# Agent attention with a mixture of experts on one core: maxima over partitions by TensorE, scores and routing products later in TensorE's order, keys spread over three quarters of a batch, low halves on GpSimd

## The chip, the cores and the metric

The kernel runs on one core of a Trainium2 chip. The metric is the device time of one execution in microseconds (us), the median over several runs. A core has five engines that each work through a queue of their own in order: TensorE (PE in the rows; PEld is its weight load), VectorE (DVE), ScalarE (ACT), GpSimd (POOL) and SyncE (SP, which here issues nearly all DMAs). They wait for each other by semaphores.

## The reference

```python
def attn(q, k, v, agents):              # q, k, v: (4, 11456, 128); agents: (4, 49, 128)
    scale = 1 / sqrt(128)
    a2k = softmax(scale * agents @ k.T)     # each agent over all 11456 keys
    agent_v = a2k @ v
    q2a = softmax(scale * q @ agents.T)     # each query over the 49 agents
    return q2a @ agent_v                    # x: 4*11456 = 45824 tokens of 128

def moe(x, expert_emb, tau, w1, w2):    # 8 experts, w1 (8, 128, 1024), w2 (8, 1024, 128)
    logits = normalize(x) @ normalize(expert_emb).T / tau
    e = argmax(logits); gate = softmax(logits)[e]
    return gate * (relu(x @ w1[e]) @ w2[e])   # top 1
```

All inputs and the output are float32 in DRAM.

## The kernel before

**Units and steps.** A batch of 11456 tokens is cut into 12 units of 1024 tokens (128 partitions by 8 columns; the last unit is 96 by 2). Two tiles of 512 tokens make a unit, 23 tiles a batch. The expert network (FFN) takes a tile in 8 slices of 128 of its 1024 hidden channels. A slice of a tile is a **step**: 184 steps a batch, 736 in all. In step i TensorE makes the hidden slice `hp` by two fp16 products (L698, L699: high and low part of the weights, 512 columns each), ScalarE writes its rectified high half `hh` (L702), VectorE the low half `hl` (L703), and four steps later (LAG) twelve products of 128 columns bring `hh` and `hl` into the output `yp` (L720 to L722). After eight steps VectorE multiplies `yp` by the gate (`ot`, L735) and SP stores it (L741).

**Key, value and query units** are worked beside the steps. `split` (L278) prepares a key or query unit: ScalarE squares and sums it (L284), VectorE makes a power of two from the sum (`half_scale`, `hsc`, L158 to L162), then the unit is written as a high and a low fp16 half, and SP transposes both by DMA (L299) into `kT` or `qT`. The high half is made by ScalarE (L291) or, in the way "P" of `LO_BY`, by GpSimd (L289). The low half is made by VectorE in one operation (L296) or, in the way "p", by GpSimd in two (L293, L294). While the FFN runs, keys take the ways p, d, P in turn, and queries p and P. `scores` (L302) then makes 24 small products (tile `sp`, 49 columns each). For a key unit ScalarE copies the scores to `s_u` (L338) and VectorE brings them into the running maximum `m_run` (L342). When all twelve are done, `k_max` (L396) takes the maximum over a partition's columns (VectorE, L399) and then over the partitions (`allred`, GpSimd, L135: tile `pm`). `k2_unit` then subtracts `pm` (`kd`, L382: by VectorE in the first batch, by GpSimd in the later ones), takes the exponential on ScalarE (L384), and TensorE sums the values by it (`avp`, L388). A query unit goes from its scores through L545, L547, an exponential (L549), two fp16 halves (L553, and `e` on GpSimd, L554) and a DMA transpose (L556) to `tt`, the tile that both the routing products (`rtp`, L565) and the FFN read. `rt`, `quad` and `nrm` (L590 to L622) give the tokens' norms and gates.

**Order.** Each unit is a generator; a number that it yields is a delay in steps. `spawn` starts one, `keys` (L993) starts the key and value units of batch b+1 while batch b is in the FFN (the table `W_` gives the stretches of a batch in which keys and values are started), `queries` (L1031) starts one query unit for every two tiles, four units ahead. The tile framework's scheduler then puts the emitted instructions into an order for each engine, with the FFN's at higher priority. Input units lie in the pool `ld` (8 buffers), split and transposed units in three buffers each (`xs`, `xT`). The first batch's keys, values and four queries come before step 0 (`first`), and of the keys every second unit is worked in fp32. Before step 0 no unit of the ways p and P is made. The expert of a batch is chosen on the chip from its first query unit (`e0i`), and SP reads it into a register before it loads the weights (`load_expert`, L526): all DMAs that stand behind in SP's queue wait for that.

Of the kernel before, what the change touches and what calls it, by code (L numbers as in the profile page):

```python
# [31 lines left out]
def kernel(ctx: ExitStack, tc: tile.TileContext, q, k, v, agents, emb, tau, w1, w2, out):  # L32
# [35 lines left out]
    ld = ctx.enter_context(tc.tile_pool(name="ld", bufs=8))  # L68
# [63 lines left out]
    def allred(col, n, tag, op=ROP.max, bufs=2):  # L132

        r = sm.tile([P, n], F32, name="pm", tag=tag, bufs=bufs)
        pool.partition_all_reduce(r, col, P, op)  # L135
        return r
# [37 lines left out]
    def now_run(g):  # L174

        while True:
            try:
                next(g)
            except StopIteration as s:
                return s.value  # L180

# [3 lines left out]
    sga, isga = now_run(pow2(allred(amx, 1, "amxr"), 10, "sga"))  # L185
# [92 lines left out]
    def split(kind, b, u, g):  # L278

        s = units[kind, b, u]  # L280
        p, n = ushape(u)
        sq = sm.tile([P, 1], F32, name="usq", tag=kind + "usq", bufs=3)[:p]
        xs = wk.tile([P, UJ, 2, D], F16, name=kind + "s", tag="xs", bufs=3)
        act.activation(xs[:p, :n, 0], s[:p, :n], AF.Square, accum_out=sq)  # L284
        yield g
        sc, iv = yield from half_scale(sq, 14, kind + "u", 4, escale if kind == "q" else None)
        lo = LO_BY[kind][u % len(LO_BY[kind])] if ffn_at[0] is not None else "d"
        if lo == "P":
            pool.tensor_tensor(out=xs[:p, :n, 0], in0=s[:p, :n], in1=sc.unsqueeze(2).broadcast_to([p, n, D]), op=ALU.mult)  # L289
        else:  # L290
            act.activation(xs[:p, :n, 0], s[:p, :n], AF.Copy, scale=sc)  # L291
        if lo == "p":
            pool.tensor_tensor(out=s[:p, :n], in0=s[:p, :n], in1=sc.unsqueeze(2).broadcast_to([p, n, D]), op=ALU.mult)  # L293
            pool.tensor_tensor(out=xs[:p, :n, 1], in0=s[:p, :n], in1=xs[:p, :n, 0], op=ALU.subtract)  # L294
        else:
            dve.scalar_tensor_tensor(out=xs[:p, :n, 1], in0=s[:p, :n], scalar=sc, in1=xs[:p, :n, 0],  # L296
                                     op0=ALU.mult, op1=ALU.subtract)
        xT = wk.tile([P, 2 * UJ, P], F16, name=kind + "T", tag="xT", bufs=3)
        sp.dma_start_transpose(out=xT[:, : 2 * n, :p], in_=xs[:p, :n].rearrange("p c h d -> p (c h d)"))  # L299
        return xT, iv  # L300
# [27 lines left out]
    def k1_unit(b, u, g, cp):  # L328
        kb = blk_of(b, u)
        p, n = ushape(u)  # L330
        while ("k", b, u) not in units:
            yield 1
        xT, iv = yield from split("k", b, u, g[0])
        yield g[1]
        spv = scores(b, u, xT)
        st = wk.tile([P, UJ, A], F32, name="s_u", tag="s_u", bufs=NU)[:p, :n]
        if cp is act:
            act.activation(st, spv, AF.Copy, scale=iv)  # L338
        else:
            dve.tensor_scalar(st, spv, iv, None, ALU.mult)  # L340
        yield g[2]
        dve.tensor_tensor(out=kb.m_run[:p, :n, :], in0=kb.m_run[:p, :n, :], in1=st, op=ALU.max)  # L342
        kb.s[u] = st
        kb.k1 += 1

    def k1_f32(b, u):
# [4 lines left out]
        kT = wk.tile([P, 2 * UJ, P], F16, name="kT", tag="xT", bufs=3).rearrange("k c p -> k (c p)").bitcast(F32)  # L351
# [15 lines left out]
        act.activation(st, s[:p, : n * A].rearrange("p (c a) -> p c a", a=A), AF.Copy, scale=sga[:p])  # L367
        dve.tensor_tensor(out=kb.m_run[:p, :n, :], in0=kb.m_run[:p, :n, :], in1=st, op=ALU.max)
# [27 lines left out]
    def k_max(b, i=0):  # L396
# [3 lines left out]
        kb.m = allred(m1, A, "kmax", bufs=max(2, NB))  # L400
# [543 lines left out]
    def first():  # L944
# [11 lines left out]
        for kind, b, u in ops:  # L956
# [7 lines left out]
            if kind == "k":  # L964
                if not hasattr(batches[b], "blks"):
                    k_start(b)
                spawn(k1_f32(b, u) if b == 0 and u in KF else k1_unit(b, u, (0, 1, 0), act))
# [9 lines left out]
            elif kind == "m":  # L977
# [4 lines left out]
                k_max(0, i)  # L982
# [10 lines left out]
    def keys():  # L993
# [3 lines left out]
        W_ = [(0, 0.2, 0.2, 0.7), (-0.2, 0.0, 0.3, 0.85), (-0.2, 0.0, 0.3, 0.85)]  # L997
# [8 lines left out]
        for i, (at, kind, b, u) in enumerate(ops):  # L1006
# [104 lines left out]
```

## Time and profile before

| | |
|---|---|
| median of 3 runs | 1204.39 us (1203.04 to 1204.79) |
| the profiled execution: its time, its span | 1205.41 us, 1203.6 us |
| PE busy, mean granted clock | 86%, 0.958 of full speed |
| DVE, ACT, POOL busy | 75%, 57%, 36% |
| share of the 16 DMA engines | 55% |
| step 0 of the FFN | about 110 us after the start |

The rows further down come from the trace of the profiled execution; their times count from the start of its span. A row of a timeline ends with the idle time of the engine just before that instruction and, behind an arrow, the instruction whose end it waited for. [...]

### The profile page before, as it was taken

The numbers are of one execution on the slowest core, as the hardware profiler recorded it, in microseconds if no ns is written. First come the engines' busy times: TensorE is split into PE (matmuls) and PEld (weight loads), VectorE is DVE, ScalarE is ACT, GpSimd is POOL, SyncE is SP. The second block draws the span as 40 slices with busy tenths as digits, with TensorE's granted clock in tenths as the row PEclk, the third lists the DMA queues.
The fourth block names the chain that finished last, engine by engine and source line by source line (L and its number), as shares of the span: only waits on it lengthen the run. The fifth ranks groups of instructions, "written<-read, shape, count | busy, mean of one in ns | idle before, by whom it ended". The sixth has DMA issues, their size and how long they took to land. (4 is left out here: it accounts for less than half of the span.)

```text
span 1203.6 us, 34100 instructions
## 1 busy us (share of the span) xinstructions
PE 1036.3 (86%) x13877; PEld 844.2 (70%) x13877; DVE 903.1 (75%) x2103; ACT 686.9 (57%) x1304; POOL 430.0 (36%) x409
## 2 busy tenths in 40 slices
PE   2666876698999877799998987689999989999998
PEld 2664655577787765587887776568788867877776
DVE  2555787567688896788778887686778998777785
ACT  2434676455647765555755676555554575655553
POOL 2002665445401644733442343733331262252200
PEclk9887898899999999899999999899999999999999
DMA  4976999465225988554542699753330382241100
GB/s 143 249 143 209 226 200 206 106 159 128 68 60 199 205 202 192 123 119 111 140 137 54 151 236 204 158 98 96 100 73 28 91 208 68 93 92 46 39 37 32
DMA packets 302697, 157.35 MB, mean 131 GB/s; under 512 B 227067, under 2 KB 279371, under 8 KB 302539
## 3 DMA queue, kind: packets, MB, share of 16 engines
q1 hardware_dynamic: 302475, 155.16, 54.4%
q8 instruction: 109, 1.79, 0.6%
q14 instruction: 49, 0.40, 0.1%
q0 software_dynamic: 64, 0.00, 0.0%
HBM read 75.80 MB, written 23.53 MB: 83 GB/s over the span
## 5 line engine op out<-in xcount | busy, mean ns | idle before, releaser
L703 DVE SCALAR_TENSOR_TENSOR hl<-hp,hh 128x512 f16<-128x512 f32 (+1 forms) x736 | 475.5, 666 | 95.9 <-ACT hh L702 86.2
L702 ACT ACTIVATE hh<-hp 128x512 f16<-128x512 f32 (+1 forms) x736 | 414.8, 584 | 217.0 <-PE yp L721 95.1
L720 PE MATMUL yp<-w2h,hh 128*128 128x128 f16 (+1 forms) x2880 | 528.5, 222 | 6.2 <-DVE ot L735 6.2
L721 PE MATMUL yp<-w2l,hh 128*128 128x128 f16 (+1 forms) x2880 | 529.0, 222 | 1.9 <-DVE w2l L516 1.9
L722 PE MATMUL yp<-w2h,hl 128*128 128x128 f16 (+1 forms) x2880 | 528.8, 222 | 0.0
L698 PE MATMUL hp<-tt,gh 128*128 128x512 f16 (+1 forms) x736 | 277.8, 378 | 66.1 <-DVE hl L703 60.4
L720 PEld LDWEIGHTS <-hh 128*128 128x128 f16 (+1 forms) x2880 | 288.0, 100 | 50.8 <-issue 3.3
L722 PEld LDWEIGHTS <-hl 128*128 128x128 f16 (+1 forms) x2880 | 287.8, 100 | 49.8 <-issue 6.2
L721 PEld LDWEIGHTS <-hh 128*128 128x128 f16 (+1 forms) x2880 | 288.1, 100 | 46.3 <-issue 8.5
L699 PE MATMUL hp<-tt,gl 128*128 128x512 f16 (+1 forms) x736 | 278.0, 378 | 0.3 <-DVE gl L507 0.3
L699 PEld LDWEIGHTS <-gl 128*128 128x128 f16 x736 | 72.0, 98 | 78.3 <-issue 73.1
L591 POOL TENSOR_TENSOR rt<-rt,qe 128x392 f32<-128x392 f32 (+1 forms) x48 | 49.7, 1036 | 158.6 <-ACT rt L590 158.6
L388 PE MATMUL avp<-vt,kd 128*98 128x129 f32 x720 | 98.1, 282 | 7.8 <-issue 7.8
L554 POOL TENSOR_TENSOR e<-qe,e 128x392 f16<-128x392 f32 (+1 forms) x48 | 41.7, 868 | 175.3 <-DVE e L553 134.6
L388 PEld LDWEIGHTS avp<-vt,kd 128*98 128x98 f32 x720 | 88.2, 170 | 14.0 <-issue 8.3
L284 ACT ACTIVATE qs<-qt 128x1024 f16<-128x1024 f32 (+1 forms) x48 | 48.2, 1005 | 62.0 <-DMA qt<-in_q_dram 29.4
L698 PEld LDWEIGHTS <-gh 128*128 128x128 f16 x736 | 72.4, 98 | 4.4 <-issue 0.7
L622 POOL TENSOR_TENSOR nrm<-quad,half 128x16 f32<-128x16 f32 (+2 forms) x28 | 68.3, 2440 | 2.2
L158 DVE TENSOR_SCALAR hsc<-usq 128x1 int32<-128x1 int32 x90 | 13.1, 147 | 73.4 <-ACT qs L284 50.3
L735 DVE TENSOR_TENSOR ot<-yp,gs 128x512 f32<-128x512 f32 (+1 forms) x92 | 61.4, 668 | 6.6 <-PE yp L722 6.5
L284 ACT ACTIVATE ks<-kt 128x1024 f16<-128x1024 f32 (+1 forms) x42 | 42.5, 1012 | 40.0 <-DMA kT<-ks 16.0
L384 ACT ACTIVATE kd<-kd,escale 128x392 f32<-128x392 f32 (+1 forms) x48 | 28.1, 597 | 61.3 <-POOL kd L382 54.6
(252 smaller groups left out, 1520.1 us busy)
## 6 DMA issues: line engine op xcount, KB each, us to landing
kt<-in_k_dram SPq DMA_DIRECT2D x44, 512.0 KB, 4.9
vt<-in_v_dram SPq DMA_DIRECT2D x44, 512.0 KB, 4.5
qt<-in_q_dram SPq DMA_DIRECT2D x44, 512.0 KB, 4.2
out_dram<-ot SPq DMA_DIRECT2D x88, 256.0 KB, 2.3
w1s<-in_moe_w_dram SPq DMA_DIRECT2D x5, 512.0 KB, 3.8
w2s<-in_moe_w_dram SPq DMA_DIRECT2D x5, 512.0 KB, 4.7
qT<-qs SPq DMA_TRANSPOSE x48, 4.7
tt<-e SPq DMA_TRANSPOSE x48, 3.4
```

The lines of the kernel that those rows point to most:

```text
L284: act.activation(xs[:p, :n, 0], s[:p, :n], AF.Square, accum_out=sq)
L388: pe.matmul(out=avp[: 2 * A, :W], lhsT=de[:p, c * A : (c + 2) * A], rhs=src[:p, c, :], start=(c == 0), stop=(c == n - 1))
L591: pool.tensor_tensor(out=rt, in0=rt, in1=e, op=ALU.mult)
L622: pool.tensor_tensor(out=nrm, in0=quad[:, :n], in1=half[:, :n], op=ALU.pow)
L698: pe.matmul(out=hp[:, :m], lhsT=bt.gh[:, fs], rhs=tt, start=True, stop=False)
L699: pe.matmul(out=hp[:, :m], lhsT=bt.gl[:, fs], rhs=tt, start=False, stop=True)
L702: act.activation(hh[:, :m], hp[:, :m], AF.Relu)
L703: dve.scalar_tensor_tensor(out=hl[:, :m], in0=hp[:, :m], scalar=0.0, in1=hh[:, :m], op0=ALU.max, op1=ALU.subtract)
L720: pe.matmul(out=y, lhsT=hh[:, cs], rhs=bt.w2h[:, f, :], start=(f == 0 and c == 0), stop=False, skip_group_check=True)
L721: pe.matmul(out=y, lhsT=hh[:, cs], rhs=bt.w2l[:, f, :], start=False, stop=False, skip_group_check=True)
L722: pe.matmul(out=y, lhsT=hl[:, cs], rhs=bt.w2h[:, f, :], start=False, stop=last, skip_group_check=True)
L735: dve.tensor_tensor(out=o[:p, :n], in0=yp[:p, :n], in1=gate, op=ALU.mult)
```

## The change

Five things change together.

- **Maxima over partitions.** `allred` (GpSimd) is replaced by `allmax`: TensorE transposes the column maxima into PSUM (`mT`, new L142), VectorE reduces them along the row (`mTx`, L144), a step passes, a product of TensorE spreads them to all partitions (`mB`, L147), ScalarE copies them out (`pm`, L149). All nine uses change: the agents' absolute maximum, the three blocks of the first batch's keys, `k_max` of the other three batches, and `count_strays`, which runs twice.
- **Halves.** While the FFN runs, every high half is made by ScalarE (new L293) and every low half by GpSimd in two operations (L295, L296); `LO_BY` is gone. VectorE makes low halves only before step 0.
- **The keys' running maximum** is taken by VectorE straight from the scores in PSUM, scaled in the same operation, and no longer reads ScalarE's copy.
- **Delays and places.** The scores of a key or query stand 7 steps behind the split (before 4), the routing products 6 steps behind the transpose (before 4). Keys of batches 2 and 3 are started from half a batch ahead of the place where batch b-1 begins to a quarter behind it (before: the last fifth of the batch ahead); values from 0.3 to 0.8.
- **Buffers.** `xs` and `xT` have five buffers (before three), `ld` eleven (before eight); queries load one unit further ahead.

```diff
-    LO_BY = {"k": "pdP", "q": "pP"}
     LAG = 4
+    XB = 5
-    ld = ctx.enter_context(tc.tile_pool(name="ld", bufs=8))
+    ld = ctx.enter_context(tc.tile_pool(name="ld", bufs=11))
-    def allred(col, n, tag, op=ROP.max, bufs=2):
+    def allmax(col, n, tag, psx, g, bufs=2):
+
+        t_ = psx("mT")
+        pe.transpose(out=t_[:n, :P], in_=col, identity=ident)
+        mx = sm.tile([P, 1], F32, name="mTx", tag="mTx")[:n]
+        dve.tensor_reduce(out=mx, in_=t_[:n, :P], axis=AX.X, op=ALU.max)
+        yield g
+        t_ = psx("mB")
+        pe.matmul(out=t_[:, :n], lhsT=mx.broadcast_to([n, P]), rhs=ident[:n, :n], start=True, stop=True)
         r = sm.tile([P, n], F32, name="pm", tag=tag, bufs=bufs)
-        pool.partition_all_reduce(r, col, P, op)
+        act.copy(r, t_[:, :n])
         return r
...
-    sga, isga = now_run(pow2(allred(amx, 1, "amxr"), 10, "sga"))
+    sga, isga = now_run(pow2(now_run(allmax(amx, 1, "amxr", pss, 0)), 10, "sga"))
...
-        xs = wk.tile([P, UJ, 2, D], F16, name=kind + "s", tag="xs", bufs=3)
+        xs = wk.tile([P, UJ, 2, D], F16, name=kind + "s", tag="xs", bufs=XB)
...
-        lo = LO_BY[kind][u % len(LO_BY[kind])] if ffn_at[0] is not None else "d"
-        if lo == "P":
-            pool.tensor_tensor(out=xs[:p, :n, 0], in0=s[:p, :n], in1=sc.unsqueeze(2).broadcast_to([p, n, D]), op=ALU.mult)
-        else:
-            act.activation(xs[:p, :n, 0], s[:p, :n], AF.Copy, scale=sc)
-        if lo == "p":
+        act.activation(xs[:p, :n, 0], s[:p, :n], AF.Copy, scale=sc)
+        if ffn_at[0] is not None:
             pool.tensor_tensor(out=s[:p, :n], in0=s[:p, :n], in1=sc.unsqueeze(2).broadcast_to([p, n, D]), op=ALU.mult)
             pool.tensor_tensor(out=xs[:p, :n, 1], in0=s[:p, :n], in1=xs[:p, :n, 0], op=ALU.subtract)
...
-    def k1_unit(b, u, g, cp):
+    def k1_unit(b, u, g):
...
-        if cp is act:
-            act.activation(st, spv, AF.Copy, scale=iv)
-        else:
-            dve.tensor_scalar(st, spv, iv, None, ALU.mult)
-        yield g[2]
-        dve.tensor_tensor(out=kb.m_run[:p, :n, :], in0=kb.m_run[:p, :n, :], in1=st, op=ALU.max)
+        act.activation(st, spv, AF.Copy, scale=iv)
+        mr = kb.m_run[:p, :n, :]
+        dve.scalar_tensor_tensor(out=mr, in0=spv, scalar=iv, in1=mr, op0=ALU.mult, op1=ALU.max)
...
-        W_ = [(0, 0.2, 0.2, 0.7), (-0.2, 0.0, 0.3, 0.85), (-0.2, 0.0, 0.3, 0.85)]
+        W_ = [(0, 0.25, 0.3, 0.8), (-0.5, 0.25, 0.3, 0.8), (-0.5, 0.25, 0.3, 0.8)]
...
-                spawn(k1_unit(b, u, (1, 4, 1), act))
+                spawn(k1_unit(b, u, (1, 7)))
...
-                    k_max(b)
-                    yield 2
+                    yield from k_max(b, pss, 1)
+                    yield 1
...
-                unit_load(q, "q", b, u)
-                spawn(q_unit(b, u, (1, 4, 1, 1, 4, 2)), 3)
+                for i in (b * NU + u, b * NU + u + 1):
+                    unit_load(q, "q", i // NU, i % NU)
+                spawn(q_unit(b, u, (1, 7, 1, 1, 6, 2)), 3)
```

How the orders change is shown at three places. First GpSimd's queue where the key maximum of batch 2 is due (about 476 us in the trace of before); `ISA` is an instruction without a shape, `pm` the maximum. Before:

```order
L294 TENSOR_TENSOR qs<-qt,qs 128x8x128
L135 ISA
L135 ISA pm<-m_8364 128x49
L289 ISA
L289 TENSOR_TENSOR qs<-qt,hsc 128x8x128
L382 TENSOR_TENSOR kd_129<-s_u,pm 128x392
L382 TENSOR_TENSOR kd_130<-s_u,pm 128x392
```

The same place in the changed kernel:

```order
L296 TENSOR_TENSOR qs<-qt,qs 128x8x128
L592 TENSOR_TENSOR rt<-rt,qe 128x392
L618 TENSOR_SCALAR quad<-quad 128x16
L623 TENSOR_TENSOR nrm<-quad,half 128x16
L383 TENSOR_TENSOR kd_135<-s_u,pm 128x392
L383 TENSOR_TENSOR kd_136<-s_u,pm 128x392
L383 TENSOR_TENSOR kd_137<-s_u,pm 128x392
```

The maximum and both `ISA` without a tile are gone from the queue; the changed kernel has such a row only at the very start, ahead of the identity matrix.

Second SP's queue behind the load of batch 1's expert, where batch 2's keys begin in the kernel before (about 381 us):

```order
L116 DMA kt<-in_k_dram 128x1024 x3
L741 DMA out_dram<-ot 128x512
L116 DMA kt<-in_k_dram 128x1024
L299 DMA_TRANSPOSE kT<-ks 128x16x128
L116 DMA kt<-in_k_dram 128x1024
L741 DMA out_dram<-ot 128x512
L116 DMA qt<-in_q_dram 128x1024
L556 DMA_TRANSPOSE tt<-e_1_133 128x8x128
L116 DMA kt<-in_k_dram 128x1024 x2
L299 DMA_TRANSPOSE qT<-qs 128x16x128
L299 DMA_TRANSPOSE kT<-ks 128x16x128 x2
```

In the changed kernel, from the same load on:

```order
L115 DMA kt<-in_k_dram 128x1024
L115 DMA qt<-in_q_dram 128x1024
L115 DMA kt<-in_k_dram 128x1024 x2
L115 DMA qt<-in_q_dram 128x1024
L115 DMA kt<-in_k_dram 96x256
L115 DMA qt<-in_q_dram 128x1024
L115 DMA vt<-in_v_dram 128x8x128
L115 DMA qt<-in_q_dram 128x1024
L742 DMA out_dram<-ot 128x512
L115 DMA vt<-in_v_dram 128x8x128
L301 DMA_TRANSPOSE kT<-ks 128x16x128
```

Before, seven key loads stand in these rows, two more ahead of them behind the same register read, with a small one ten of the batch's twelve; now four are left behind that read, and the other eight stand ahead of it. Queries and values stand there in their place.

Third GpSimd's queue at the FFN's first steps (from 110 us). Before:

```order
L289 TENSOR_TENSOR qs<-qt,hsc 128x8x128
L289 TENSOR_TENSOR ks<-kt,hsc 128x8x128
L293 TENSOR_TENSOR kt<-kt,hsc 128x1024
L294 TENSOR_TENSOR ks<-kt,ks 128x8x128
L293 TENSOR_TENSOR qt<-qt,hsc 128x1024
L294 TENSOR_TENSOR qs<-qt,qs 128x8x128
L554 TENSOR_TENSOR e_1_133<-qe,e_1_133 128x8x49
```

Between its second and third `e` the changed kernel has:

```order
L296 TENSOR_TENSOR qs<-qt,qs 128x8x128
L295 TENSOR_TENSOR kt<-kt,hsc 128x1024 x2
L295 TENSOR_TENSOR qt<-qt,hsc 128x1024
L296 TENSOR_TENSOR ks<-kt,ks 128x8x128
L295 TENSOR_TENSOR kt<-kt,hsc 128x1024
L592 TENSOR_TENSOR rt<-rt,qe 128x392
L296 TENSOR_TENSOR ks<-kt,ks 128x8x128
L296 TENSOR_TENSOR qs<-qt,qs 128x8x128
L555 TENSOR_TENSOR e_0_138<-qe,e_0_138 128x8x49
```

Single operations on high halves became pairs: ahead of the fourth `e` there were 5 pairs and 4 single ones and are now 13 pairs; ahead of the eighth, 8 pairs and 9 single ones and now 27 pairs.

## Rows read from the trace of the kernel before

**Rows 1.** The page: busy time of the engines, share of the span, instructions.
```profile
PE 1036.3 (86%) x13877; PEld 844.2 (70%) x13877; DVE 903.1 (75%) x2103; ACT 686.9 (57%) x1304; POOL 430.0 (36%) x409
```

**Rows 2.** Windows, line L698 alone (one per step): stretch, length, busy, clock, DMA share, GB/s.
```profile
109.00:237.00 128.00, 25.41 (x65) 6.54 (x65) 0.90 0.89 199
237.00:381.00 144.00, 36.55 (x96) 9.31 (x95) 0.99 0.44 110
381.00:495.00 114.00, 23.95 (x64) 6.33 (x64) 0.93 0.84 196
495.00:675.00 180.00, 48.44 (x128) 12.45 (x128) 1.00 0.48 115
675.00:806.00 131.00, 30.48 (x81) 8.06 (x81) 0.95 0.81 177
1128.00:1181.00 53.00, 18.28 (x49) 4.79 (x49) 1.00 0.09 33
```

**Rows 3.** Windows, tile sp (score products): PE, PEld, DVE and ACT busy first.
```profile
381.00:495.00 114.00, 12.43 (x366) 0.00 (x0) 4.44 (x8) 6.79 (x12) 0.93 0.84 196
675.00:806.00 131.00, 13.05 (x366) 0.00 (x0) 6.55 (x12) 5.60 (x10) 0.95 0.81 177
```

**Rows 4.** Timeline of PE at three places: start, duration, instruction, idle before and releaser.
```profile
233.03 0.58 PE L698 MATMUL hp<-tt,gh 128*128 128x512 f16 x1 [8.29 <-DVE hl L703]
...
488.68 0.59 PE L698 MATMUL hp<-tt,gh 128*128 128x512 f16 x1 [10.76 <-DVE hl L703]
...
758.06 0.59 PE L698 MATMUL hp<-tt,gh 128*128 128x512 f16 x1 [8.64 <-DVE hl L703]
```

**Rows 5.** Timeline of POOL and of ACT at the second of these places.
```profile
475.87 0.52 POOL L135 PARTITION_ALL_REDUCE pm<-m  x1 [5.64 <-DVE hiv L165]
484.15 1.88 POOL L289 TENSOR_TENSOR qs<-qt,hsc 128x1024 f16<-128x1024 f32 x1 [7.76 <-issue]
486.01 2.83 POOL L382 TENSOR_TENSOR kd<-s_u,pm 128x392 f32<-128x392 f32 x2
...
486.98 0.62 ACT L384 ACTIVATE kd<-kd,escale 128x392 f32<-128x392 f32 x1 [8.44 <-POOL kd L382]
```

**Rows 6.** Waits of PE over the whole run: us in total, times, longest.
```profile
PE hp L698 <- DVE hl L703: 60.4, 32, 10.8
PE sp L308 <- DMA kT<-ks: 11.8, 7, 3.1
```

**Rows 7.** Lines of the halves and of the maximum: count, shortest/median/longest ns.
```profile
L293 POOL TENSOR_TENSOR kt<-kt,hsc x12: 1892/1899/2613, 120.6 to 711.8; 128x1024 f32<-128x1024 f32 x12
L293 POOL TENSOR_TENSOR qt<-qt,hsc x23: 1882/1893/2897, 125.4 to 1062.5; 128x1024 f32<-128x1024 f32 x23
L294 POOL TENSOR_TENSOR ks<-kt,ks x12: 2127/2232/3120, 123.3 to 714.5; 128x1024 f16<-128x1024 f32 x12
L291 ACT ACTIVATE ks<-kt,hsc x30: 1133/1148/1181, 15.7 to 718.3; 128x1024 f16<-128x1024 f32 x30
L296 DVE SCALAR_TENSOR_TENSOR qs<-qt,hsc,qs x25: 471/1276/3162, 74.7 to 1069.8; 128x1024 f16<-128x1024 f32 x21, 96x256 f16<-96x256 f32 x4
L342 DVE TENSOR_TENSOR m_run<-m_run,s_u x42: 241/558/2254, 32.7 to 739.7; 128x392 f32<-128x392 f32 x39, 96x98 f32<-96x98 f32 x3
L545 DVE TENSOR_REDUCE qmx<-sp x48: 244/555/568, 90.6 to 1134.6; 128x8 f32<-128x392 f32 x44, 96x2 f32<-96x98 f32 x4
```

**Rows 8.** Costliest groups on the page: POOL's other work per query unit.
```profile
L591 POOL TENSOR_TENSOR rt<-rt,qe 128x392 f32<-128x392 f32 (+1 forms) x48 | 49.7, 1036 | 158.6 <-ACT rt L590 158.6
L554 POOL TENSOR_TENSOR e<-qe,e 128x392 f16<-128x392 f32 (+1 forms) x48 | 41.7, 868 | 175.3 <-DVE e L553 134.6
L622 POOL TENSOR_TENSOR nrm<-quad,half 128x16 f32<-128x16 f32 (+2 forms) x28 | 68.3, 2440 | 2.2
```

**Rows 9.** Timeline of POOL, DVE and ACT at the start, around the agents' maximum.
```profile
25.67 0.38 POOL L135 PARTITION_ALL_REDUCE pm<-amx  x1 [5.96 <-DMA kt<-in_k_dram]
...
26.08 0.15 DVE L143 TENSOR_SCALAR p2c<-pm 128x1 f32<-128x1 f32 x1 [6.52 <-POOL pm L135]
...
26.58 1.15 ACT L291 ACTIVATE ks<-kt,hsc 128x1024 f16<-128x1024 f32 x1 [8.19 <-DVE hsc L160]
```

More of the change, by code (lines that the diff above doesn't have):

```diff
@@ L130, with now_run @@
         dve.tensor_copy(aT_all[:, b, :], t_[:, :A])
-    def allred(col, n, tag, op=ROP.max, bufs=2):
+    def now_run(g):
+        while True:
+            try:
+                next(g)
+            except StopIteration as s:
+                return s.value
+    def allmax(col, n, tag, psx, g, bufs=2):
[6 more added lines that the diff above has]
+        pe.matmul(out=t_[:, :n], lhsT=mx.broadcast_to([n, P]), rhs=ident[:n, :n], start=True, stop=True)
         r = sm.tile([P, n], F32, name="pm", tag=tag, bufs=bufs)
-        pool.partition_all_reduce(r, col, P, op)
+        act.copy(r, t_[:, :n])
         return r
@@ L172, in total @@
         return s
[L174 to L180, printed above, removed]
     amx = cst.tile([P, 1], F32, name="amx")
     dve.tensor_reduce(out=amx, in_=aT_all, axis=AX.XY, op=ALU.max, apply_absolute_value=True)
-    sga, isga = now_run(pow2(allred(amx, 1, "amxr"), 10, "sga"))
+    sga, isga = now_run(pow2(now_run(allmax(amx, 1, "amxr", pss, 0)), 10, "sga"))
     escale = cst.tile([P, 1], F32, name="escale")
@@ L297, in split @@
                                      op0=ALU.mult, op1=ALU.subtract)
-        xT = wk.tile([P, 2 * UJ, P], F16, name=kind + "T", tag="xT", bufs=3)
+        xT = wk.tile([P, 2 * UJ, P], F16, name=kind + "T", tag="xT", bufs=XB)
         sp.dma_start_transpose(out=xT[:, : 2 * n, :p], in_=xs[:p, :n].rearrange("p c h d -> p (c h d)"))
@@ L350, in k1_f32 @@
         src = units["k", b, u]
-        kT = wk.tile([P, 2 * UJ, P], F16, name="kT", tag="xT", bufs=3).rearrange("k c p -> k (c p)").bitcast(F32)
+        kT = wk.tile([P, 2 * UJ, P], F16, name="kT", tag="xT", bufs=XB).rearrange("k c p -> k (c p)").bitcast(F32)
         for c0 in range(0, n, TJ):
@@ L366, in k1_f32 @@
         st = wk.tile([P, UJ, A], F32, name="s_u", tag="s_u", bufs=NU)[:p, :n]
-        act.activation(st, s[:p, : n * A].rearrange("p (c a) -> p c a", a=A), AF.Copy, scale=sga[:p])
-        dve.tensor_tensor(out=kb.m_run[:p, :n, :], in0=kb.m_run[:p, :n, :], in1=st, op=ALU.max)
+        spv = s[:p, : n * A].rearrange("p (c a) -> p c a", a=A)
+        act.activation(st, spv, AF.Copy, scale=sga[:p])
+        mr = kb.m_run[:p, :n, :]
+        dve.scalar_tensor_tensor(out=mr, in0=spv, scalar=sga[:p], in1=mr, op0=ALU.mult, op1=ALU.max)
         kb.s[u] = st
@@ L394, in k2_unit, with k_max @@
         kb.k2 += 1
-    def k_max(b, i=0):
+    def k_max(b, psx, g, i=0):
         kb = batches[b].blks[i]
@@ L399, in k_max @@
         dve.tensor_reduce(out=m1, in_=kb.m_run.rearrange("p c a -> p a c"), axis=AX.X, op=ALU.max)
-        kb.m = allred(m1, A, "kmax", bufs=max(2, NB))
+        kb.m = yield from allmax(m1, A, "kmax", psx, g, bufs=max(2, NB))
     def k_weights(b):
@@ L746, in count_strays @@
     def count_strays():
-        cur = allred(cnt_p, NG, "cntr")
+        cur = yield from allmax(cnt_p, NG, "cntr", pss, 1)
         yield 2
@@ L966, in first @@
                     k_start(b)
-                spawn(k1_f32(b, u) if b == 0 and u in KF else k1_unit(b, u, (0, 1, 0), act))
+                spawn(k1_f32(b, u) if b == 0 and u in KF else k1_unit(b, u, (0, 1)))
             elif kind == "v":
@@ L981, in first @@
                     yield 1
-                k_max(0, i)
+                now_run(k_max(0, psh, 0, i))
                 if i == NB - 1 and NB > 1:
```

## The prediction

> **What bounds the kernel now.** The page comes first: TensorE is busy 86% of the span, VectorE 75%, ScalarE 57%, GpSimd 36% [rows 1]. So TensorE's own work is nearest to the end, and the question is where it stands still or is slowed. The windows by step rate tell: in the last stretch, where nothing but the FFN is left, 49 steps take 53.00 us, 1.08 us a step; in the calm stretch 495 to 675 us it is 180/128 = 1.41 us, with the clock at 1.00 and the DMA engines 48% busy. But in 109 to 237 us a step costs 128/65 = 1.97 us, in 381 to 495 us 114/64 = 1.78, in 675 to 806 us 131/81 = 1.62, with the DMA share at 0.81 to 0.89 and the clock at 0.90 to 0.95 [rows 2]. The second and third are the stretches in which the keys of batches 2 and 3 come.
>
> What these two lose: 64 steps at 1.08 are 69 us, and the score products 12.4 us; 114 - 69 - 12 - 2 (routing products, an estimate) leaves 31 us. In the third, 131 - 87.5 - 13 leaves 30 [rows 2, 3]. The timeline of PE shows one piece of each: the FFN stands for 10.76 and 8.64 us, and for 8.29 us once more at 233 us, in the first stretch, each time for VectorE's `hl`; the product after it lasts 0.58 us [rows 4]. Following the second wait back: GpSimd takes the maximum at 475.87, idle 5.64 us before it, and its next operation starts at 484.15 after 7.76 us in which it waited for nothing that the profile shows; `kd` comes behind, ScalarE stands 8.44 us for it, its `hh` and so `hl` come late [rows 5]. So a maximum on GpSimd costs two idle times on its queue, some 13 us, and the three of the later batches cost TensorE 8.29 + 10.76 + 8.64 = 27.7 us [rows 4]. All waits of the FFN for `hl` are 60.4 us in 32 places [rows 6], so nearly half lie there.
>
> **The change part by part.**
>
> *The maximum.* The order shows nothing between GpSimd's other work and `kd` any more. What replaces it are four short operations on TensorE, VectorE and ScalarE, each in a queue that turns over within a step or two (some 2 to 3 us in all by the step rates above). `kd` waits for them, but ahead of it GpSimd now has some 6 us of pairs and query work, so it comes to `kd` no sooner than `pm` does. I take the whole 27.7 us back. The lower end is 20: what 2.5 us of chain would leave at each of the three places. Nothing speaks for a loss beyond that except the queues, below.
>
> [...]
>
> *Keys spread over three quarters of a batch.* Outside the maxima the two bursts lose 31 - 10.8 = 20 and 30 - 8.6 = 22, together 42 us. In the changed order eight of batch 2's twelve keys stand ahead of the register read, in the stretch where a step took 1.50 us and DMA was 44% busy [rows 2], four behind it. The score products go along; they cost the same anywhere. But queries and values have moved up behind the same read, and by my count nine units still come close together there, again in the third batch. Either end is open: 0 us if the bunch is as bad as before, 42 if the loss goes with the keys. I take half, -21.
>
> *The first steps.* Ahead of the eighth output store (step 64) SP's order has now three loads and three transposes of key and query units more, and one transpose of `tt` fewer. At 199 GB/s [rows 2] each 0.52 MB move is 2.6 us, so 5.5 moves are 14.5 us of DMA in a stretch where the engines are 89% busy. TensorE waits there for other things too, so not all of it shows; I take +10, between 0 and +14.5.
>
> *Low halves on GpSimd.* About 83 pairs in place of 35, at 4.1 us, and 36 single operations less, at 1.9: GpSimd's 430 us [rows 1] become some 560, half the span. Up to unit 7's `e` it has 27 pairs, 111 us, and with eight `e`, seven `rt`, three `nrm` and three `kd` some 25 more [rows 8]: 136 us. That `e` is needed at step 112, which came at 237 + 47 × 1.50 - 109 = 198 us after step 0 [rows 2]. So GpSimd is 70% busy there, and it holds. Nothing on the path pays. VectorE loses some 49 operations of 1.28 us, and its running maximum leaves SBUF's two operands for one in PSUM; ScalarE gains 36 of 1.15 us [rows 7] at 57% busy. What was queued behind these long operations was `hl`: of the other 32.7 us of waits for it I give back 4 (an eighth; 0 to 10). Cover for the pairs is GpSimd's 30% idle time; without it each pair costs its whole 4.1 us.
>
> *Delays and buffers.* With scores 3 steps later and five buffers, TensorE's 11.8 us for `kT` [rows 6] should shrink; I count nothing (0 to -6), since the delay also brings `tt` 5 steps nearer to its use.
>
> *The start.* The agents' maximum no longer waits for 5.96 us of GpSimd. VectorE stood 6.52 us and ScalarE 8.19 us there [rows 9]; loads run on underneath, so I take -4 (0 to -6.5), and +1 for the chain of four at the first batch's third block, +1 for the new small products on TensorE.
>
> **Sum**: -27.7 - 21 + 10 - 4 - 4 + 1 + 1 = -44.7. From the profiled execution's 1205.4 that is 1160.7; the median of the runs is 1.0 us below that execution, so **1160 us**.
>
> **Rivals.**
>
> *The bursts stay* (0.20). The DMA share of 0.81 to 0.84 in both bursts [rows 2] may mean that the data, not the order, sets the pace, and spreading moves the loss into the stretches that were calm. Against it: over the span the engines are far from full, and the calm stretch moves 115 GB/s where a burst moves 196 [rows 2]. Then the maxima alone count: 1205.4 - 27.7 less 1 to 5 for the start, so 1173 to 1178; with +10 at the first steps, up to 1188.
>
> *GpSimd becomes the bound* (0.12, the one that ends slower). Every pair now passes through one queue ahead of `e`, and `tt` waits for `e`. The slowest rows of the two operations are 2.90 and 3.12 us [rows 7], a pair of 6.0. At that price unit 7's 27 pairs are 163 us, with 25 and gaps no less than the 198 that there are, so it decides from about 6 us a pair. Each then costs 1.9 more than my 4.1: 27 of them +51, the bursts keep their 42 instead of 21 (+21), which gives 1160 + 72 = 1232; half of it, 1196, if only the first steps suffer. What speaks for it: VectorE's operation with two operands in SBUF goes from 558 to 2254 ns while the one that reads PSUM stays within 568 [rows 7], so something is shared. Against: the medians are at the short end.
> [...]
>
> *The first batch gains too* (0.10). If five buffers and the later scores free the first steps as well, their excess (128 - 65 × 1.41 = 36 us against the calm rate) shrinks by a third instead of growing by 10: 1160 - 12 - 10 = 1138, and with both bursts gone 1117.
>
> *The change doesn't do what it says* (0.04). The chain through four queues costs as much as the idle times did, and the order bunches as before: within 0.2% of 1204.
>
> **How the numbers follow.** The forecast has 0.54: 1143 to 1175 by the half of the bursts that is open (±15). Differences under 0.2%, 2.4 us, can hardly be told from none here. Faster are the forecast, the bursts that stay, and the first batch's gain: 0.54 + 0.20 + 0.10 = 0.84; the same 0.04; slower 0.12. For 8 in 10 the range takes the forecast's own, most of the bursts that stay, and the nearer half of the larger gain: 1126 to 1192.
>
> **What would show it.** GpSimd's timeline has no idle time near 6 to 8 us without a releaser beside a maximum, and PE's waits for `hl` drop from 60.4 to about 30 with none above 6 us. The step rate in the places of the two bursts comes to 1.5 to 1.6 us, in the calm ones it stays near 1.4 to 1.45. The first steps take more than 128 us for 65. A GpSimd pair stays below 4.5 us in the mean. Wrong I am if waits of `rtp` for `tt`, or of `e`'s transpose for GpSimd, grow beyond 30 us (GpSimd is then the bound), if the bursts merely change place, or if the first steps come down to 1.6 us each.

## The result and the profile after

The changed kernel takes 1165.45 us (median of 4 runs, 1163.57 to 1169.28) where the kernel before took 1203.72 us in runs on the same chips (1198.08 to 1204.79): a ratio of 0.9695 with a 95% interval of 0.9654 to 0.9737 (it is the ratio of the means; the two medians alone give 0.968). The forecast was 1160 us, so the sum came out within 6 us. That is in part luck: several of its terms were off, and the two largest errors went opposite ways.

The page's row of busy times, for [rows 1]:

```profile
PE 1037.0 (89%) x13904; PEld 843.4 (72%) x13904; DVE 865.2 (74%) x2064; ACT 714.7 (61%) x1349; POOL 523.0 (45%) x460
```

The span of this execution is 1167.5 us: TensorE does the same work in 36 us less. Next the windows of one product per step (now L699), cut near the places of the stretches in [rows 2]. The first two hold the same steps as there, the last three 80, 113 and 96 where they held 64, 128 and 81. Columns as there:

```profile
98.00:230.00 132.00, 25.98 (x65) 6.60 (x64) 0.85 0.95 209
230.00:383.00 153.00, 36.54 (x96) 9.38 (x96) 0.99 0.59 133
383.00:498.00 115.00, 30.12 (x80) 8.02 (x80) 0.97 0.89 207
498.00:661.00 163.00, 42.40 (x113) 10.90 (x112) 1.00 0.50 115
661.00:796.00 135.00, 35.96 (x96) 9.43 (x96) 0.97 0.70 163
```

The steps begin 11.7 us earlier. The first 65 take 132 us instead of 128, the next 96 take 153 instead of 144. The two bursts are gone as such: 115/80 = 1.44 and 135/96 = 1.41 us a step, where there were 1.78 and 1.62, although the DMA engines are as busy in the first of them (0.89) as before (0.84). Over the same steps the gain is a little smaller than these rates say: by the table below 1.64 to 1.45 us a step for steps 160 to 239, and 1.59 to 1.41 for 352 to 447.

TensorE's waits over the run, for [rows 6]:

```profile
PE rtp L566 <- DMA tt<-e: 33.7, 16, 15.5
PE hp L699 <- DVE hl L704: 30.8, 35, 3.2
...
PE yp L721 <- DVE ot L736: 7.0, 1, 7.0
```

Waits for `hl` fell from 60.4 to 30.8 us and none is above 3.2. Waits of the routing products for `tt` became the largest, one of them 15.5 us long. The queue of GpSimd where batch 2's maximum arrives, for [rows 5]:

```profile
502.33 2.93 POOL L623 TENSOR_TENSOR nrm<-quad,half 128x16 f32<-128x16 f32 x1
505.58 2.81 POOL L383 TENSOR_TENSOR kd<-s_u,pm 128x392 f32<-128x392 f32 x3 [0.31 <-ACT pm L149]
```

No idle time of 6 to 8 us is left there; GpSimd waits 0.31 us for `pm`. That the chain of four operations takes long does not matter: VectorE's maximum over a partition's columns starts at 486.88 us, and `pm` is copied at 505.31, so it comes some 18 us later, not the 2 to 3 I had put down, but GpSimd reaches `kd` no sooner: ahead of it in its queue it works, or waits 5.04 and 4.82 us for VectorE and ScalarE.

The start shows what I missed. GpSimd's timeline in the kernel before has this row:

```profile
13.99 0.28 POOL masks.py:199 TENSOR_SCALAR_AFFINE_SELECT ident<-ident 128x128 f32<-128x128 f32 x1 [12.14 <-issue]
```

The same instruction in the timeline of the changed kernel:

```profile
1.91 0.29 POOL masks.py:199 TENSOR_SCALAR_AFFINE_SELECT ident<-ident 128x128 f32<-128x128 f32 x1
```

The identity matrix, which every transpose by TensorE needs, is there 12 us earlier, and TensorE's first product starts at 5.05 us instead of 14.33.

And here is the longest wait, in the windows of 153 to 176 us (PE, PEld, DVE, ACT, POOL busy, clock, DMA share, GB/s) and the timelines of PE, of GpSimd and of SP:

```profile
153.00:176.00 23.00, 8.84 (x132) 5.75 (x129) 13.70 (x36) 17.64 (x31) 23.00 (x18) 0.75 1.14 234
...
178.69 0.23 PE L566 MATMUL rtp<-r_hi,tt 128*128 128x58 f16 x1 [15.47 <-DMA tt<-e]
...
168.13 0.90 POOL L555 TENSOR_TENSOR e<-qe,e 128x392 f16<-128x392 f32 x1
...
172.78 2.85 SPq L557 DMA_TRANSPOSE tt<-e  x1
```

GpSimd is busy for all of these 23.00 us and TensorE for 8.84 of them. The `e` that TensorE waits for, the fourth unit's, comes at 168.13 us in that stretch without a gap; SP issues its transpose 3.75 us after it is done. TensorE stands at step 41, seven steps ahead of that unit's own first FFN step (48).

To compare stretches between kernels I take the time from the start of a step's first product to that of another's, and, as its loss, that time less TensorE's own pace (products in the stretch by the distance between the starts of neighbours that nothing holds up: 0.216 us for 512 columns, 0.056 for 128, 0.026 for a score product, 0.027 for a routing product, 0.11 for most of the others). The last column runs to the end of the steps' last product. In us, loss in brackets (the last five rows give times alone), each row from the one profiled execution:

| kernel | step 0 at | steps 0-63 | 64-159 | 160-239 | 240-351 | 352-447 | 448-735 |
|---|---|---|---|---|---|---|---|
| before | 109.6 | 127.2 (47) | 144.5 (11) | 131.6 (34) | 162.5 (9) | 153.0 (31) | 369.6 (14) |
| changed | 97.9 | 129.8 (51) | 154.4 (16) | 115.6 (19) | 162.7 (6) | 135.3 (18) | 365.5 (10) |
| maxima only | 97.1 | 115.8 (37) | 145.2 (11) | 129.7 (29) | 162.2 (11) | 147.3 (25) | 366.5 (11) |
| changed, old places | 96.9 | 123.9 (46) | 142.9 (8) | 126.3 (26) | 154.7 (4) | 143.6 (20) | 358.3 (3) |
| changed, old halves | 95.9 | 124.1 (44) | 143.5 (8) | 116.2 (19) | 164.2 (8) | 135.8 (18) | 365.3 (9) |
| changed, old buffers | 98.9 | 113.7 (36) | 157.9 (20) | 114.7 (16) | 171.0 (16) | 135.1 (17) | 365.8 (10) |
| changed, `e` on VectorE | 94.0 | 122.2 (42) | 147.8 (12) | 117.6 (20) | 161.9 (6) | 135.4 (18) | 366.4 (10) |
| all but the maxima | 107.8 | 126.3 | 154.3 | 131.1 | 164.3 | 144.4 | 367.1 |
| before, new places | 108.6 | 119.6 | 166.9 | 128.6 | 173.8 | 142.7 | 368.0 |
| before, new halves | 108.7 | 117.7 | 156.9 | 133.9 | 162.0 | 155.1 | 367.6 |
| changed, old halves and buffers | 94.7 | 111.5 | 152.3 | 114.7 | 170.4 | 133.9 | 368.1 |
| the same, old places too | 97.5 | 118.1 | 141.0 | 121.2 | 161.2 | 149.5 | 376.5 |

### The profile page after: what moved, and what is told of

Read it like the earlier page. It is cut to its first block, busy times and chain, and to the rows that moved or that the text cites. A ratio compares the mean times of both kernels' runs of the same rounds, so it can differ in the third digit from the quotient of the medians.

```text
span 1167.5 us, 34151 instructions
## 1 busy us (share of the span) xinstructions
PE 1037.0 (89%) x13904; PEld 843.4 (72%) x13904; DVE 865.2 (74%) x2064; ACT 714.7 (61%) x1349; POOL 523.0 (45%) x460
## 4 chain that ended last, share of the span: by engine, by line
PE 50%; DMA 14%; DVE 11%; issue 10%; POOL 8%; ACT 5%; SPq 1%; ACTq 0%; POOLq 0%; DVEq 0%
PE hp L699 8%; PE hp L700 8%; PE yp L722 8%; PE yp L723 8%; PE yp L721 8%; PE avp L389 5%; DVE hl L704 4%; DMA kT<-ks 4%; DMA tt<-e 3%; DMA kt<-in_k_dram 3%; DMA qT<-qs 2%; POOL qt L295 2%; POOL ks L296 2%; POOL qs L296 2%; ACT hh L703 1%
## 5 line engine op out<-in xcount | busy, mean ns | idle before, releaser
L722 PE MATMUL yp<-w2l,hh 128*128 128x128 f16 (+1 forms) x2880 | 523.6, 220 | 2.0 <-DVE w2l L517 2.0
L723 PE MATMUL yp<-w2h,hl 128*128 128x128 f16 (+1 forms) x2880 | 523.1, 220 | 0.0
L723 PEld LDWEIGHTS <-hl 128*128 128x128 f16 (+1 forms) x2880 | 285.8, 99 | 48.1 <-issue 5.0
L699 PE MATMUL hp<-tt,gh 128*128 128x512 f16 (+1 forms) x736 | 278.4, 378 | 35.7 <-DVE hl L704 30.8
L295 POOL TENSOR_TENSOR qt<-qt,hsc 128x1024 f32<-128x1024 f32 (+1 forms) x47 | 85.8, 1829 | 75.8 <-ACT qs L293 70.3
L295 POOL TENSOR_TENSOR kt<-kt,hsc 128x1024 f32<-128x1024 f32 (+1 forms) x36 | 64.5, 1795 | 70.1 <-ACT ks L293 70.1
L296 POOL TENSOR_TENSOR qs<-qt,qs 128x1024 f16<-128x1024 f32 (+1 forms) x47 | 94.4, 2012 | 0.7
L592 POOL TENSOR_TENSOR rt<-rt,qe 128x392 f32<-128x392 f32 (+1 forms) x48 | 46.3, 965 | 100.6 <-ACT rt L591 100.4
L172 DVE TENSOR_SCALAR hsc<-usq 128x1 int32<-128x1 int32 (+1 forms) x90 | 13.4, 149 | 84.5 <-ACT qs L290 45.1
L699 PEld LDWEIGHTS <-gh 128*128 128x128 f16 x736 | 72.7, 99 | 3.7 <-issue 1.4
L296 POOL TENSOR_TENSOR ks<-kt,ks 128x1024 f16<-128x1024 f32 (+1 forms) x36 | 72.4, 2012 | 0.8
```

What stands on the lines that cost most here:

```text
L592: pool.tensor_tensor(out=rt, in0=rt, in1=e, op=ALU.mult)
L699: pe.matmul(out=hp[:, :m], lhsT=bt.gh[:, fs], rhs=tt, start=True, stop=False)
L722: pe.matmul(out=y, lhsT=hh[:, cs], rhs=bt.w2l[:, f, :], start=False, stop=False, skip_group_check=True)
L723: pe.matmul(out=y, lhsT=hl[:, cs], rhs=bt.w2h[:, f, :], start=False, stop=last, skip_group_check=True)
```

## The experiments

All ratios are to the kernel before, run beside it on the same chip, with 95% intervals. That kernel's median was 1209.82 us beside the first four runs, 1205.01 beside the next four and 1209.42 beside the last four, so between such groups the ratios compare and the times do not. No run undoes the keys' running maximum from PSUM by itself; what it is worth is not shown.

**Maxima alone.** The kernel before with `allmax` at all nine places.

```diff
-        pool.partition_all_reduce(r, col, P, op)
...
+        pe.transpose(out=t_[:n, :P], in_=col, identity=ident)
...
+        dve.tensor_reduce(out=mx, in_=t_[:n, :P], axis=AX.X, op=ALU.max)
+        yield g
...
+        pe.matmul(out=t_[:, :n], lhsT=mx.broadcast_to([n, P]), rhs=ident[:n, :n], start=True, stop=True)
...
+        act.copy(r, t_[:, :n])
```

> The kernel before with all nine maxima over partitions by TensorE and nothing else of the change. Theory A (the maxima are nearly the whole gain: the trace after has step 0 of the FFN 11.7 us earlier, and the three stalls of 8.29, 10.76 and 8.64 us gone, 39 us together, while the other parts cancel): 1163 to 1172 us. Rival B (the other parts carry their share, and part of the earlier start is lost again in the DMA-bound first steps): 1178 to 1190 us.

Measured: 1171.72 us, ratio 0.970 [0.9659, 0.9741]. That is the whole change's ratio; theory A holds. TensorE's longest wait for `hl` is 4.0 us here. Of the 34 us by which its profiled execution is shorter, 12.5 lie ahead of step 0; the three stretches with the stalls (steps 0-63, 160-239, 352-447) lose 21 us less between them, not 27.7.

**All but the maxima.** The changed kernel with `partition_all_reduce` back at the nine places.

> The changed kernel with every maximum back on GpSimd. Theory A: the gain is gone, 1195 to 1210 us, with idle times of 5 to 8 us on GpSimd's queue around each maximum and step 0 again near 110 us. Rival B (the spread keys gain by themselves what I forecast, 21 us, less the first steps): 1180 to 1194 us.

Measured: 1197.07 us, 0.988 [0.9853, 0.9906]: within A's range in time, but clearly better than before. Without the new maxima the rest of the change is worth 1.2%; with them, nothing. Step 0 stands at 107.8 us. The two bursts (steps 160-239 and 352-447) take 131.1 and 144.4 us here, 129.7 and 147.3 with the maxima alone, and 115.6 and 135.3 in the changed kernel: neither side brings them down by much, both together do.

**Places alone, halves alone**, each on the kernel before.

```diff
-        W_ = [(0, 0.2, 0.2, 0.7), (-0.2, 0.0, 0.3, 0.85), (-0.2, 0.0, 0.3, 0.85)]
+        W_ = [(0, 0.25, 0.3, 0.8), (-0.5, 0.25, 0.3, 0.8), (-0.5, 0.25, 0.3, 0.8)]
```

> The kernel before with the new table of places for keys and values alone. Theory A (the loss of the two bursts outside the stalls fell by 9 us in the trace after, not by my 21): 1192 to 1200 us. Rival B (my forecast of half the loss): 1180 to 1187 us. Rival C (it needs the buffers and later scores to go with it): 1201 to 1215 us.

Measured: 1.0027 [0.9996, 1.0058], 1214.32 us. Neither A nor B: the spread alone brings nothing. The time lies in C's range, but C's reason is not borne out: all but the maxima has the spread together with the buffers and the later scores, and its bursts stay at 131.1 and 144.4 us. What the spread needs beside it, by these runs, are the new maxima.

```diff
-        lo = LO_BY[kind][u % len(LO_BY[kind])] if ffn_at[0] is not None else "d"
...
+        act.activation(xs[:p, :n, 0], s[:p, :n], AF.Copy, scale=sc)
+        if ffn_at[0] is not None:
```

> The kernel before with every high half on ScalarE and every low half on GpSimd in pairs once the FFN runs, and nothing else. Theory A (GpSimd's queue makes the halves e of the queries late in the first steps, where the trace after shows one wait of 15.5 us for tt): 1206 to 1220 us, most of it lost before step 64. Rival B (VectorE's relief outweighs it, as I forecast with 4 us): 1196 to 1203 us.

Measured: 0.9959 [0.9937, 0.9982], 1207.06 us where the kernel before took 1209.82 beside it. The time lies in A's range, the ratio says a small gain, as B has it; the first 64 steps take 117.7 us, 10 less than before. But steps 64 to 159 take 156.9, 12 more, since the stall for `hl` has only moved from step 63 to step 75 (7.48 us). Over both stretches the pairs cost 3 us here, and no wait of `rtp` for `tt` is above 3.7 us.

**Undoing one part of the changed kernel each.**

```diff
-        W_ = [(0, 0.25, 0.3, 0.8), (-0.5, 0.25, 0.3, 0.8), (-0.5, 0.25, 0.3, 0.8)]
+        W_ = [(0, 0.2, 0.2, 0.7), (-0.2, 0.0, 0.3, 0.85), (-0.2, 0.0, 0.3, 0.85)]
```

> The changed kernel with the old table of places for keys and values. Ratios are to the kernel before; the changed kernel stands at 0.9695. Theory A (the spread helps the two bursts by about 13 us once the stalls are gone, as the losses of batch 2's and 3's bursts in the maxima-only trace against the changed kernel's show): 0.976 to 0.984. Rival B (the spread is a wash here as it was alone on the kernel before, ratio 1.003): 0.965 to 0.973.

Measured: 1158.93 us, 0.9597 [0.9534, 0.9659]. Both miss: old places gain here. By the table they give 9 us back to the bursts' losses, but take 13 off those of the first 160 steps and 7 off the last.

```diff
-        act.activation(xs[:p, :n, 0], s[:p, :n], AF.Copy, scale=sc)
-        if ffn_at[0] is not None:
+        lo = LO_BY[kind][u % len(LO_BY[kind])] if ffn_at[0] is not None else "d"
+        if lo == "P":
...
```

> The changed kernel with the old division of high and low halves. Theory A (GpSimd's pairs ahead of the queries' e are what the first 64 steps pay, about 14 us more than with the maxima alone): 0.955 to 0.963 of the kernel before, with no wait for tt above 8 us. Rival B (the pairs' relief for VectorE is worth as much as they cost, and the first steps are slow for their DMA): 0.966 to 0.976, and the long wait for tt stays.

Measured: 1152.82 us (1151.84 to 1155.48), 0.9543 [0.9483, 0.9603], the lowest ratio of all kernels here and below both ranges, A's by less than 0.1 points. Its waits of `rtp` for `tt` are 19.1 us, the longest 5.1. Theory A holds. From step 160 on its stretches are those of the changed kernel within 2 us; the pairs on GpSimd cost 17 us in the first 160 steps and gain nothing later.

```diff
-                spawn(k1_unit(b, u, (1, 7)))
+                spawn(k1_unit(b, u, (1, 4)))
...
-                spawn(q_unit(b, u, (1, 7, 1, 1, 6, 2)), 3)
+                spawn(q_unit(b, u, (1, 4, 1, 1, 4, 2)), 3)
```

> The changed kernel with scores 4 steps behind the split and routing products 4 behind the transpose, as before. Theory A (the delay gives DMA and GpSimd time, and without it TensorE stands for kT and qT again, 20 us of such waits before): 0.975 to 0.985 of the kernel before. Rival B (the later scores cost as much in late tt): 0.963 to 0.973.

Measured: 1170.29 us, 0.9681 [0.9617, 0.9744]: rival B, the delays make no difference that shows.

```diff
-    XB = 5
+    XB = 3
...
-    ld = ctx.enter_context(tc.tile_pool(name="ld", bufs=11))
+    ld = ctx.enter_context(tc.tile_pool(name="ld", bufs=8))
```

> The changed kernel with three xs and xT buffers and eight load buffers. Theory A (more buffers let SP run ahead, which in the DMA-bound first steps puts loads and transposes in front of tt; without them the first steps are shorter, but scores 7 steps later hold the three buffers): within 0.5 per cent of the changed kernel, 0.965 to 0.975 of the kernel before. Rival B (buffers carry the later scores): 0.98 to 1.0.

Measured: 1163.74 us, 0.9615 [0.9553, 0.9677]: a little below A's range, far from B's, and overlapping the changed kernel's interval. The table shows why the sum stands still: 15 us less loss in the first 64 steps, 14 us more in steps 64 to 159 and 240 to 351. (Queries still load one unit further ahead in this run.) Every pair and every `e` is on GpSimd here too, and yet TensorE hardly waits for `tt`:

```profile
PE rtp L566 <- DMA tt<-e: 8.9, 11, 1.3
```

With three buffers 16 pairs stand ahead of the sixth unit's `e` instead of 21, and it is done 105 us after step 0 instead of 123. So the late `tt` of the changed kernel takes both: the pairs, and the buffers that let more of them run ahead of `e`.

**Which way the pairs cost time.** The changed kernel, pairs and all, with the queries' low half `e` on VectorE.

```diff
-        pool.tensor_tensor(out=e2[:p, :n, LO : LO + A], in0=e, in1=hi, op=ALU.subtract)
+        dve.tensor_tensor(out=e2[:p, :n, LO : LO + A], in0=e, in1=hi, op=ALU.subtract)
```

> The changed kernel with the low half e of the queries' exponentials on VectorE instead of GpSimd, so that it no longer stands behind the pairs in GpSimd's queue; the pairs themselves stay. Theory A (the pairs cost time by holding up e in that queue): waits of rtp for tt fall from 33.7 us to under 20, 0.955 to 0.964 of the kernel before. Rival B (the pairs cost time by holding up VectorE's operations on two SBUF operands, as in the one of 7.02 us at 180.55, or by the later transposes of the units): waits stay above 25 us or move to hl, 0.967 to 0.980.

Measured: 1160.22 us, 0.9597 [0.958, 0.9615], and of TensorE's waits:

```profile
PE rtp L566 <- DMA tt<-e: 21.4, 14, 5.0
```

Theory A in time, with its bound for the waits just missed: those for `tt` fall from 33.7 to 21.4 us and the longest from 15.5 to 5.0 with every pair still on GpSimd; those for `hl` rise from 30.8 to 37.1. The old halves gave 1.5%, this gives 1.0%; so the larger part of the pairs' cost is, as far as the intervals tell, `e` standing behind them in one queue. In the first 160 steps it is 14 of the 17 us. (The execution profiled took 1152.96 us, the fastest of five; the others took about 1160.)

When `e` is done, in us after step 0, for the second to seventh unit:

| kernel | 2nd | 3rd | 4th | 5th | 6th | 7th |
|---|---|---|---|---|---|---|
| before | 21 | 34 | 58 | 77 | 91 | 128 |
| changed | 27 | 45 | 71 | 96 | 123 | 149 |
| changed, old halves | 25 | 38 | 59 | 78 | 97 | 124 |
| changed, `e` on VectorE | 28 | 43 | 66 | 87 | 101 | 118 |
| changed, old buffers | 24 | 45 | 68 | 88 | 105 | 126 |

**A late use of the old reduction.** The changed kernel with only the two maxima of `count_strays`, far from the start, back on GpSimd.

```diff
+    def allred(col, n, tag, op=ROP.max, bufs=2):
...
-        cur = yield from allmax(cnt_p, NG, "cntr", pss, 1)
+        cur = allred(cnt_p, NG, "cntr")
```

> The changed kernel with only the two maxima of count_strays back on GpSimd (about 926 and 1161 us in the trace before, where nothing on the path waited for them). Theory A (the idle 12.1 us at the start of GpSimd's queue, which delayed TensorE's first work from 7 to 14 us, belongs to a program that uses this reduction anywhere): step 0 of the FFN again near 108 us, 0.977 to 0.985 of the kernel before, with the 12 us of idle time ahead of the identity matrix. Rival B (it belongs to the early uses alone): step 0 stays at 97 to 99 us, 0.966 to 0.973.

Measured: 1176.87 us, 0.9741 [0.972, 0.9763], step 0 at 104.0 us, and on GpSimd:

```profile
13.03 0.28 POOL masks.py:199 TENSOR_SCALAR_AFFINE_SELECT ident<-ident 128x128 f32<-128x128 f32 x1 [11.18 <-issue]
...
904.67 0.45 POOL L142 PARTITION_ALL_REDUCE pm<-cnt_p  x1 [6.00 <-DVE lr L435]
```

The program's first use of the reduction is at 904.67 us, and still the identity matrix waits 11.18 us at the start. Theory A in its mechanism: the idle time belongs to the program, not to the early uses. In time it lies between the two: the ratio 0.3 points below A's range and 0.1 above B's, step 0 at 104.0 us. Of the 11.7 us about 6 come back; that the rest stays away because the agents' maximum keeps its new form is a guess that no run separates.

**Together.** Old halves with old buffers, and those with old places as well.

> The changed kernel with the old division of halves (0.954 of the kernel before on its own) and the old buffers (0.9615 on their own; the first 64 steps took 113.7 us with them instead of 129.8, the next 96 157.9 instead of 154.4). Theory A (both take load off the first steps by ways of their own, GpSimd's queue and SP's running ahead, so they add up in part): 0.942 to 0.951 of the kernel before. Rival B (both cure the same late tt, so the second adds nothing): 0.952 to 0.960.

Measured: 1154.39 us, 0.9566 [0.952, 0.9613]: rival B, no more than old halves alone. The first 64 steps fall to 111.5 us, but 64 to 159 take 152.3 and 240 to 351 take 170.4.

> The changed kernel with old halves, old buffers and old places: what is left of the change is the maxima by TensorE, the later scores and routing products, and the keys' running maximum straight from PSUM. Theory A (spread keys help the two bursts by about 13 us and the other two parts only harm the first steps): 0.955 to 0.965 of the kernel before, slower than without the old places. Rival B (old places are no worse, as in the changed kernel, where they gained 1 per cent): 0.940 to 0.952.

Measured: 1169.97 us, 0.9665 [0.9635, 0.9695], slower by 1.0 point than with the new places; nearer to A, a little beyond its range. With old halves and buffers the spread helps; with the new halves and buffers it harms (0.9597 without it, 0.9695 with). The traces agree on most of it. In both pairs the spread takes some 20 us off the two bursts (19 and 22) and adds some 20 to steps 64-159 and 240-351 (20 and 21): the loss moves. The sign comes from the first 64 steps and those from 448 on, 13 us more with the new halves and buffers and 15 less with the old ones. Each row is a single execution, though: of the four of its kernel the fastest for the changed kernel with old places, and the slowest for the last row. (In the last two kernels, too, queries load one unit further ahead, which the expectation leaves out of what is left of the change.)

## Why the prediction came out right, point by point

- **The stalls, -27.7.** Right in place: with the maxima alone the longest wait for `hl` is 4.0 us where there were 8.29, 10.76 and 8.64 [rows 4]. The size was too large: there the three stretches lose 21 us less, near the lower end of 20, and all waits for `hl` fall from 60.4 to 48.1 us. That this run reaches the whole change's ratio it owes to the start as well.
- **The start, -4 and +1.** The term was mis-sized: step 0 comes 11.7 us earlier (12.5 with the maxima alone). I had read the 6.5 us behind `pm` [rows 9] and taken the 12.14 us ahead of the identity matrix for something that both kernels pay, since the row `ISA` stands there in both orders. The order shows that an instruction is there, not what it takes; with the late use alone it takes 11.18 us again.
- **Keys spread, -21.** Mis-sized: outside the stalls the two bursts lost 34 - 10.8 = 23 and 31 - 8.6 = 22 us; they lose 19 and 18 now, so 8 us are back. This split takes the stalls at their whole length, and the two terms cannot be told apart in the bursts, since each part alone does little there and both together take 28 us off (65 to 37; the sum has 10.8 + 8.6 + 21 = 40). Against the kernel with the maxima alone the gain in these stretches is 17 (54 to 37), but 19 more are lost in the first 160 steps, of which old places take 13 back. The rival "the bursts stay" named this: the loss changed place, though the bursts' rate did come down.
- **First steps, +10.** Without the stall of 8.29 us they lost 39 us; they lose 51, so +12, near the forecast. The cause was not the one I gave alone: the buffers (-15 when undone) and the pairs on GpSimd (-7) both take part.
- **Low halves on GpSimd, "it holds; nothing on the path pays".** This step failed. The pair's price was right (two operations of 1.89 and 2.13 us at the median, 4.0 together, where [rows 7] give 4.1); over the run GpSimd was 45% busy, and in the first 64 steps 76%, not far from the 70% that I had. But in the first steps it had stretches without a gap, and worked its queue in order (VectorE is done with the fourth unit's `e` at 164.13 us, GpSimd starts its part at 168.13, behind operations of two pairs): `e` of the fourth unit is done 71 us after step 0 instead of 58, that of the sixth 123 instead of 91, and `tt` and the routing products wait, 15.47 us for the fourth. I compared the unit's need at its own FFN step with the sum of the work, when the routing products that TensorE has in order earlier (step 41 against 48) already wait for it. Old halves take 1.5% off, `e` moved out of that queue 1.0%. With the old buffers the same pairs leave waits for `tt` of 8.9 us in all, so the buffers, for which I counted nothing, belong to this step too.
- **The rival on GpSimd as the bound** was conditioned on a pair of 6 us. Its consequence showed up, in part, at 4 us a pair; the condition was the wrong one.
- **Delays, 0.** Right within what can be told (0.9681 against 0.9695).
- **The signs.** Those of the maxima came true: waits for `hl` are 30.8 us, none above 3.2, and the bursts run even faster than the 1.5 to 1.6 us a step that I gave. But one sign of being wrong came true as well: waits of `rtp` for `tt` are 33.7 us, beyond the 30 that I had named. GpSimd was not the bound of the whole kernel, but of some first steps.

By the trace the sum is -11.7 (start) - 27.7 (stalls) + 12 (steps 0 to 63) + 5 (64 to 159) - 8 (bursts) - 7 (the rest) = -37, against 36 us of span. It takes the stalls at their whole length; with 21 for them the bursts and the first steps have the difference. The total fits since the start gave 9 us more than I had and the spread 13 less. What stays open: why old places gain 1.0 point with the new halves and buffers and lose 1.0 without them, and what the buffers move between the stretches. GpSimd's queue is part of the latter, as the sixth unit's `e` shows (105 us instead of 123 with the old buffers); how much is due to the places of SP's loads and transposes no run here separates.

## What to carry to other kernels

The reduction over partitions on GpSimd cost more than its own row (0.52 us between 5.64 and 7.76 us of idle time [rows 5]): look for idle time on both sides of such an operation, also where the profile names a releaser for it, and at the start of the queue too, even where the use comes late (11.18 us for a first use at 904.67). An engine that is busy for three quarters of a stretch (here 76%) can still hold up the path (here by 15.47 us) when something short and urgent stands behind long work in its queue: compare when each product is done, not how much work there is, and remember that more buffers can let more of the long work go ahead (here 21 pairs instead of 16). And when parts of a change are summed, undo each alone and try each alone: here one part made the gain, another took the bursts down only beside it, and what the rest gained and lost cancelled.

## What the runs showed of the hardware that was not expected

A reduction over partitions on GpSimd used only at 904.67 us costs 11.18 us of idle time at the start of the program; without any it is not there (the identity matrix at 1.91 us). Of the kernel before, the answer on the reduction's line has these rows, the `ISA` without a tile of the orders:

```profile
L135 POOLq MODIFY_POOL_CONFIG  x12: 1/8/13, 19.9 to 1155.2; - x12
```

They are pairs, one ahead of six of the nine uses, and these six stand behind 5.64 to 6.12 us of idle time, whatever releaser their row names. The other three uses follow nothing but MEMSETs on GpSimd since the use before them and have no such pair. A pair stands ahead of the identity matrix in both kernels, but the matrix stands behind idle time only where the program uses the reduction (12.14 us before, 11.18 with the late use, none in the changed kernel). The late use itself stands behind 6.00 us; the start's 11 to 12 us is about twice that, and no run here says why.

VectorE's row can last until a run of GpSimd's ends, without a wait that the trace names. In the changed kernel, VectorE and then GpSimd at the same moment, and TensorE behind them:

```profile
180.55 7.02 DVE L645 SCALAR_TENSOR_TENSOR el<-esa,l 128x16 f32<-128x16 f32 x1
187.60 0.25 DVE L648 RECIPROCAL gs<-el 128x16 f32<-128x16 f32 x1
...
180.29 2.12 POOL L296 TENSOR_TENSOR ks<-kt,ks 128x1024 f16<-128x1024 f32 x1
182.37 1.00 POOL L592 TENSOR_TENSOR rt<-rt,qe 128x392 f32<-128x392 f32 x1
183.34 2.11 POOL L296 TENSOR_TENSOR ks<-kt,ks 128x1024 f16<-128x1024 f32 x1
185.41 2.11 POOL L296 TENSOR_TENSOR qs<-qt,qs 128x1024 f16<-128x1024 f32 x1
...
188.90 0.26 PE L721 MATMUL yp<-w2h,hh 128*128 128x128 f16 x1 [7.00 <-DVE ot L736]
```

An operation on 16 columns with two operands in SBUF takes 7.02 us, where the median of its 20 rows is 0.17: it ends when the last of four GpSimd operations that run back to back does, at 187.5 us, and TensorE waits 7.00 us for the `ot` behind it. (The kernel before waits 6.19 us for `ot` at the same step without such a row, so the place is tight in either.) In the run with the late reduction, too, TensorE waits 7.0 us for `ot` once. In the trace of the changed kernel one more VectorE row is over 2.5 us above the median of its kind: `l`, 4.52 us at 692.55 where the median is 0.30, and it reads one tensor. The two rows end 0.04 and 0.03 us after a GpSimd row; the kernel before has no VectorE row so far above its median. So a VectorE operation can be drawn out over a whole run of operations on the other side, while my sum had counted only VectorE's relief (-4); what holds it there no run shows.
